# Two weight slots for k and q of four heads, weight loads at the end of a head, and 32-column tiles in the attention burst

## The chip, the core and the metric

The kernel runs on one core of a Trainium2 chip. The time is that of one execution on the device in microseconds (us): the median of 3 runs. TensorE is called PE here, VectorE DVE, ScalarE ACT, GpSimd POOL and SyncE SP. SP computes nothing; it issues nearly all of the DMAs, one after another, and when one of them must wait, everything behind it on SP waits too.

## What is computed

An attention over buckets, followed by two feed-forward layers (`_moe_ref`, `_moe2_ref`), for 2 batches of 768 tokens, 8 heads of 64:

```python
q_bucket = np.sum((q @ proj > 0) * powers, axis=-1)      # 6 bits per query, and per key
scores = np.where(q_bucket[..., :, None] == k_bucket[..., None, :], scale * q @ k.T, -1e9)
attn = exp(scores - max(scores)); attn = attn / (attn.sum(-1) + 1e-09)
x = (attn @ v) as tokens x 512
h = x @ w_in;  x = (h * tanh(softplus(h))) @ w_out       # 512 -> 2048 -> 512
h = x @ w_in2; out = (P(h) / Q(h)) @ w_out2              # the same sizes
```

## The kernel before

All weights come as 64-bit floats and are turned on the chip into two 32-bit parts (hi and lo); x is held in two such parts too.

**Attention** takes 16 heads one after another. The order of all its work is written out by hand: `order` gives each piece of work (by name) a slot, six slots to a head, and within a slot the pieces stand in the table's order. `run` goes through the slots; every engine then executes its own instructions in that order. In slots 0 to 5 of head h, `st(h, c)` makes scores and the exponential E for key tile c (4 matmuls, L405, then ACT L410), and `smax(h+1, c)` the row maxima of the next head (L356, then DVE L360). Slot 5 then holds PE's burst: the bucket products of head h+2 (`code_products`, L307), E times v (`pv`, L295 in `both`, six key tiles) and the sum of E over the keys (`dsum`, L440). These three are plain 32-bit matmuls; each instruction shows as two records. L307 and L295 work in column tiles of 64 (two matmuls side by side), L440 in tiles of 32 (four side by side).

The row maxima of head h+1 reach PE by a detour, called the row write here: DVE turns them (`fin_a`, L367), and `fin_b` writes them with four DMAs of 0.8 KB into one row of `qB` (L373, qB<-stt, two issued by SP, two by ACT). The first `st` matmul of head h+1 reads that row. `fin_b` is issued in slot 5, before the burst.

The other DMAs of a head, all on SP: kk<-qB 384 KB and kk<-qX 192 KB (`move_k`, `move_x`), kq<-kq 384 KB (`load`: k and q of a later head), d<-rc, cs<-dv 3 KB and R<-d 192 KB (`store`, `gather`, `spread`: the reciprocals of the sums, through DRAM), qX<-qB 192 KB (`move_h`), and in every second head vf<-v 384 KB.

**Weights of the first layer.** While attention runs, 7 of the 16 weight tiles (EARLY) are loaded and split, in 14 parts, one to a head: `ring_load` (L121, r<-w, 512 KB), `convert` on DVE (L102, L105, L108), hi and lo on POOL. Part n is converted in slot 5 + 6n (W_AT) and loaded W_LEAD slots earlier. The first SHARED tiles have no slot of their own yet, because their slots `w0` to `w2` hold k and q during attention; their parts are stored to DRAM (`ring_put`, L144, w<-r, 2 x 256 KB in slot 8 + 6n) and loaded back by `first` (L556) near the end of attention, in the slots that FIRST lists. The other parts go straight into their weight slot (`slot_split`).

The feed-forward layers then run in 96 steps; nothing of them is touched.

Of the kernel before, what the change touches and what calls it, by code (L numbers as in the profile page):

```python
# [9 lines left out]
F32 = mybir.dt.float32  # L10
# [8 lines left out]
B, H, S, D = 2, 8, 768, 64  # L19
NT, DM, DFF = B * S, H * D, 2048  # L20
NF = DFF // 128
NK = DM // 128
HALF = S // 2
# [2 lines left out]
NC = S // 128  # L26
BIG = 2.0 ** 40
NBITS = 6
EARLY, SHARED = 7, 3
FIRST = (90, 91, 92, 93), (77, 77, 83, 83), (85, 86, 89, 89)  # L30
W_AT, W_LEAD = 5, 4
POOL_LO = (("lo", 1), ("lo", 2))
ENG = dict(
    lo="dd", hi="aa", xhi="a", xlo="dd", whi="pppp", wlo="pppp",
# [12 lines left out]
def attention_moe_moe(ctx: ExitStack, tc: tile.TileContext, kq, v, proj2, cst, eye, w1, w2, ab, out):  # L47
    nc = tc.nc

    def pool(stack, name, bufs=1, **kw):  # L50
        return stack.enter_context(tc.tile_pool(name=name, bufs=bufs, **kw))
# [3 lines left out]
    wpool = pool(ctx, "w")  # L55
# [119 lines left out]
    def attention(actx, tctx):  # L175
# [22 lines left out]
        p_raw = ac.tile([128, 64], F32, tag="pr", name="pr")  # L198
# [32 lines left out]
            nc.gpsimd.memset(f32(KK[0])[32:33, 0], -1.0)  # L231
            nc.gpsimd.memset(f32(Z), 0.0)

        raws = {}

        def load(h):
            if not 0 <= h < B * H:
                return
            b, hh = divmod(h, H)
            raws[h] = wpool.tile([128, S], F32, tag=f"w{h % 3}", name="kq")  # L240
            nc.sync.dma_start(out=raws[h], in_=kq[b, hh])


# [45 lines left out]
        def qhalf(t, a):  # L289
            return t[:, a * HALF:(a + 1) * HALF]  # L290


        def both(o, w, x, start=False, stop=False):
            for a in range(2):
                nc.tensor.matmul(out=o[64 * a:64 * a + 64, 0:HALF + 2], lhsT=w, rhs=x[:, a], start=start, stop=stop)  # L295

        def halves(p):
            return p[:, :, 0:HALF]
# [4 lines left out]
        ct = {}  # L303

        def code_products(h):
            for a in range(2):
                nc.tensor.matmul(  # L307
                    out=ct[h][a][64 * a:64 * a + 64, 0:HALF], lhsT=p_raw, rhs=qhalf(raws[h], a), start=True, stop=True
                )


        def codes(h):
            if not 0 <= h < B * H:
                return
            p = [two_banks() for _ in range(1 + (h == 0))]
            ct[h] = p[0][:, 0], p[-1][:, 1]
            code_products(h)
# [97 lines left out]
        def pv(h, c):  # L415
            if not 0 <= h < B * H:
                return
            j, e = divmod(h, 2)
            if c == 0:
                pvt[h] = two_banks()[:, 0]  # L420
            both(pvt[h], VF[j % 2][:, e, c], pt[h, c], start=(c == 0), stop=(c == NC - 1))
# [104 lines left out]
        nh = B * H  # L526
        parts = [(f, s) for f in range(EARLY if wide64 else 0) for s in range(PARTS[0])]
        jobs = {}
# [8 lines left out]
        for n, p in enumerate(parts):  # L537
            i = W_AT + 6 * n
            for fn, d in ((ring_load, -W_LEAD), (convert, 0), (ring_out, 1), (ring_put, 3))[:4 if p[0] < SHARED else 3]:
                jobs.setdefault(max(0, i + d), []).append((fn, p))  # L540

        def weights(g):
            for fn in (ring_out, convert, ring_load, ring_put):
# [5 lines left out]
        def first(f, n):  # L549
# [27 lines left out]
            ("code_q", code_q, -7, 1),  # L577
            ("move_x", move_x, -7, 1),
            ("load", load, -25, 1),
            ("first", first, FIRST, -2),  # L580
            ("pv", pv, (5,) * 6, 6),
# [6 lines left out]
            ("xlo", xlo, 29, 0),  # L588
            ("weights", weights, 0, -1),
            ("gather", gather, 6, 1),  # L590
            ("spread", spread, 12, 1),
            ("load_v", load_v, -12, 0),
            ("move_h", move_h, -5, 1),
        )
        last = 6 * nh
        slots = {}
        done = set()
        for name, fn, at, per in order:
            if name == "first":
                todo = [(at[f][n] if f < SHARED else 60, (f, n)) for f in range(EARLY) for n in range(4)]  # L600
            elif name == "pair":
                todo = [(6 * h + c + 1, (h, c)) for h in range(nh) for c in at]
            elif type(at) is tuple:
                todo = [(at[c] + 6 * h, (h, c)) for h in range(nh) for c in range(per)]
            elif per > 0:
                todo = [(at + 6 * h + c, (h, c) if per > 1 else (h,)) for h in range(nh) for c in range(per)]
            elif per == 0:
                todo = [(at + 12 * j, (j,)) for j in range(nh // 2)]
            else:
                todo = [(g, (g,)) for g in range(6 * nh)]  # L610
            for g, k in todo:
                slots.setdefault(max(g, 0), []).append((name, fn, k))
# [269 lines left out]
    with tc.manual_schedule():  # L882
        nc.scalar.preload_act_table_set("natural_log_exp_and_others")
        tctx = ExitStack()
        with ExitStack() as actx:
            run, tail = attention(actx, tctx)
            run()
        with ExitStack() as mctx:
            run = moe(mctx, tctx, tail)
            run()  # L890
# [55 lines left out]
```

## Time and profile before

| | us |
|---|---|
| median of 3 runs | 745.07 (744.18 to 747.27) |
| the profiled execution | 744.9 |
| its span, first to last instruction | 743.1 |
| PE busy | 731.5 (98% of the span) |
| DVE, ACT, POOL busy | 583.5, 426.0, 128.6 |

The granted clock of PE is 1.00 throughout, so nothing here is about the clock. PE is busy almost all the time by its records, but a busy PE is not yet a PE that streams: the end of a matmul is modelled, and records overlap. Where PE stands still shows in the idle time ahead of a row, in square brackets, with what ended it. Line numbers (L295) are those of the kernel before.

### The profile page before, as it was taken

To read this page: it belongs to the slowest core of one execution; us is meant where nothing else is said; L and a number is where in the kernel's file an instruction comes from. 1 tells how busy PE (TensorE), PEld (TensorE's weight loads), DVE (VectorE), ACT (ScalarE), POOL (GpSimd) and SP (SyncE) were. 2 spreads that over 40 slices of the span, in tenths; PEclk is the share of its full clock that TensorE was granted. 3 is DMA by queue.
4 is the path that set the end of the run, shared out by engine and by line. 5 is a ranking of instruction groups with operands and counts; after the bars stand their busy time and mean duration, and the time that the engine had idled before them with its cause. 6 is when DMAs were issued, how large, how long until landed. Compare 5 with 4: busy or idle time off the path is not lost.

```text
span 743.1 us, 10799 instructions
## 1 busy us (share of the span) xinstructions
PE 731.5 (98%) x3764; PEld 579.4 (78%) x3764; DVE 583.5 (79%) x1016; ACT 426.0 (57%) x701; POOL 128.6 (17%) x105
## 2 busy tenths in 40 slices
PE   8999999999999999999999999999999999999997
PEld 5767676767678888888888888878888888888886
DVE  5778989999829995755556777499998888898886
ACT  4766676767564442312123343687877776777674
POOL 6745556565630000000000000000000000000000
PEclk9999999999999999999999999999999999999999
DMA  7766776666554353455555777300000100010001
GB/s 189 194 177 173 214 200 193 158 174 164 140 167 149 120 151 113 120 164 166 147 162 169 243 241 225 107 0 1 1 0 17 41 0 2 0 57 1 0 1 56
DMA packets 45862, 85.49 MB, mean 115 GB/s; under 512 B 7152, under 2 KB 17520, under 8 KB 45808
## 3 DMA queue, kind: packets, MB, share of 16 engines
q1 hardware_dynamic: 45304, 84.75, 38.9%
q8 instruction: 29, 0.48, 0.3%
q14 instruction: 25, 0.20, 0.1%
q10 hardware_dynamic: 504, 0.06, 0.1%
HBM read 57.77 MB, written 14.73 MB: 98 GB/s over the span
## 4 chain that ended last, share of the span: by engine, by line
PE 91%; DVE 4%; DMA 2%; issue 1%; ACT 1%; SPq 0%; POOL 0%; DVEq 0%
PE h L690 34%; PE y L708 17%; PE y L710 17%; PE s L405 9%; PE s L295 6%; PE s L356 5%; PE s L440 2%; DMA qB<-stt 1%; PE s L307 1%; PE s L324 1%; DVE qX L72 1%; DVE smt L360 1%; DMA pr<-proj 0%; DVE xl L718 0%; DVE kk L330 0%
## 5 line engine op out<-in xcount | busy, mean ns | idle before, releaser
L690 PE MATMUL h<-xh,w 128*128 128x512 f32 x768 | 204.9, 389 | 0.0
L690 PEld LDWEIGHTS h<-xh,w 128*128 128x128 f32 x768 | 144.1, 188 | 30.3 <-issue 0.3
L72 DVE TENSOR_TENSOR gl<-ep,gh 128x512 fp32r<-128x512 f32 x96 | 65.9, 686 | 66.2 <-ACT ep L734 65.4
L733 ACT ACTIVATE gh<-h 128x512 fp32r<-128x512 f32 x48 | 28.7, 599 | 150.7 <-PE h L690 137.4
L690 PE MATMUL h<-xl,w 128*128 128x512 f32 x384 | 102.6, 389 | 0.0
L360 DVE TENSOR_REDUCE smt<-s 128x1 fp32r<-128x770 f32 x90 | 86.1, 959 | 19.2 <-PE s L356 14.2
L710 PE MATMUL y<-w,gh 128*128 128x512 f32 x384 | 96.3, 389 | 0.0
L708 PE MATMUL y<-gh,w 128*128 128x512 f32 x384 | 94.8, 389 | 0.0
L430 POOL TENSOR_TENSOR es<-e,e 128x768 f32<-128x768 f32 x48 | 88.8, 1854 | 23.9 <-ACT e L410 23.7
L410 ACT ACTIVATE e<-s 128x768 f32<-128x768 f32 x96 | 77.5, 814 | 22.1 <-PE s L405 21.6
L708 PEld LDWEIGHTS y<-gh,w 128*128 128x128 f32 x384 | 72.1, 188 | 15.0
L690 PEld LDWEIGHTS h<-xl,w 128*128 128x128 f32 x384 | 72.1, 188 | 15.0
L710 PEld LDWEIGHTS y<-w,gh 128*128 128x128 f32 x384 | 72.1, 188 | 15.0
L295 PE MATMUL s<-e,vf 128*64 128x386 f32 x384 | 65.1, 488 | 0.0
L740 ACT ACTIVATE ep<-h 128x512 f32<-128x512 f32 x48 | 28.6, 595 | 52.4 <-PE h L690 52.4
L108 DVE SCALAR_TENSOR_TENSOR r<-r,t 128x256 int32<-128x256 int32 (+1 forms) x114 | 52.1, 457 | 4.8
L405 PE MATMUL s<-qB,kk 128*128 128x384 f32 x192 | 50.4, 343 | 5.4 <-DMA qB<-stt 3.5
L105 DVE SCALAR_TENSOR_TENSOR t<-r,t 128x256 int32<-128x256 int32 (+1 forms) x114 | 52.2, 458 | 3.9
L742 DVE TENSOR_TENSOR n<-n,ep 128x512 f32<-128x512 f32 x48 | 33.1, 690 | 26.9 <-ACT n L741 26.9
L295 PEld LDWEIGHTS s<-e,vf 128*64 128x64 f32 x384 | 27.4, 137 | 34.4 <-issue 34.0
L710 PE MATMUL y<-w,gl 128*128 128x512 f32 x192 | 53.3, 392 | 0.5 <-DVE gl L72 0.4
L708 PE MATMUL y<-gl,w 128*128 128x512 f32 x192 | 51.3, 389 | 0.0
(82 smaller groups left out, 1013.9 us busy)
## 6 DMA issues: line engine op xcount, KB each, us to landing
r<-w SPq DMA_DIRECT2D x100, 256.0 KB
w<-r SPq DMA_DIRECT2D x64, 128.0 KB
w<-w SPq DMA_DIRECT2D x16, 512.0 KB
r<-w SPq DMA_DIRECT2D x14, 512.0 KB
kq<-kq SPq DMA_DIRECT2D x16, 384.0 KB
kk<-qB SPq DMA_DIRECT2D x15, 384.0 KB
kk<-qX SPq DMA_DIRECT2D x16, 192.0 KB
qX<-qB SPq DMA_DIRECT2D x16, 192.0 KB
```

The lines of the kernel that those rows point to most:

```text
L72: nc.vector.tensor_tensor(out=o, in0=i, in1=f32(h), op=ALU.subtract)
L105: lambda: nc.vector.scalar_tensor_tensor(out=t, in0=r[:, :, 1], scalar=-0x40000000, in1=t, op0=ALU.bitwise_and, op1=ALU.bitwise_or),
L108: lambda: nc.vector.scalar_tensor_tensor(out=o, in0=r[:, :, 0], scalar=29, in1=t, op0=ALU.logical_shift_right, op1=ALU.bitwise_or),
L295: nc.tensor.matmul(out=o[64 * a:64 * a + 64, 0:HALF + 2], lhsT=w, rhs=x[:, a], start=start, stop=stop)
L356: nc.tensor.matmul(out=p[:, a, 0:HALF], lhsT=qB[h % NB][:, c * 128:(c + 1) * 128], rhs=qhalf(KK[h % NB][:, 0], a), start=True, stop=True,)
L360: nc.vector.tensor_reduce(out=m, in_=p[:, :, 0:HALF + 1], op=ALU.max, axis=AX.XY)
L405: nc.tensor.matmul(out=p[:, a, 0:HALF], lhsT=kk[:, c * 128:(c + 1) * 128], rhs=qq[:, a * HALF:(a + 1) * HALF], start=(i == 0), stop=(i == 1),)
L410: nc.scalar.activation(out=E[c][:, :, 0:HALF], in_=halves(p), func=ACT.Exp, scale=1.0 / D ** 0.5)
L430: nc.gpsimd.tensor_tensor(out=sums[h, c], in0=halves(pt[h, c]), in1=halves(pt[h, c + 1]), op=ALU.add)
L690: nc.tensor.matmul(out=p, lhsT=w[:, c * 128:(c + 1) * 128], rhs=x[:, c, :], start=(n == 0), stop=(n == 11))
L708: nc.tensor.matmul(out=y[m], lhsT=w[:, DM + m * 128:DM + (m + 1) * 128], rhs=g, **s)
L710: nc.tensor.matmul(out=y[m], lhsT=g[:, m * 128:(m + 1) * 128], rhs=w[:, DM:2 * DM], **s)
```

## The change

- `load` puts head h into half of one of two slots: heads 0 and 1 (mod 4) share `w0`, heads 2 and 3 share `w1`. `w2` is free from the start, so SHARED goes from 3 to 2, and tile 2 (parts 4 and 5) goes straight into its slot. FIRST loses its first entry: tile 0 takes the slots in which tile 1 was loaded, tile 1 those of tile 2.
- W_LEAD goes from 4 to 6: a part is loaded in slot 5 of the head before, behind `fin_b`, `move_k`, `move_x`, `load` and `store`, instead of slot 1. The stores (slot 8 + 6n) stay.
- `spread` (R<-d) goes from slot 0 to slot 2 of a head, behind the stores.
- `both` and `code_products` make four matmuls of 32 columns where there were two of 64.

```diff
-EARLY, SHARED = 7, 3
-FIRST = (90, 91, 92, 93), (77, 77, 83, 83), (85, 86, 89, 89)
-W_AT, W_LEAD = 5, 4
+EARLY, SHARED = 7, 2
+FIRST = (77, 77, 83, 83), (85, 86, 89, 89)
+W_AT, W_LEAD = 5, 6
...
-            raws[h] = wpool.tile([128, S], F32, tag=f"w{h % 3}", name="kq")
+            i, j = divmod(h % 4, 2)
+            if h < 4 and j == 0:
+                home[i] = wpool.tile([128, 2, 2 * DM], F32, tag=f"w{i}", name="kq")
+            raws[h] = home[i][:, j, 0:S]
...
-            for a in range(2):
-                nc.tensor.matmul(out=o[64 * a:64 * a + 64, 0:HALF + 2], lhsT=w, rhs=x[:, a], start=start, stop=stop)
+            for a in range(4):
+                nc.tensor.matmul(
+                    out=o[32 * a:32 * a + 32, 0:HALF + 2], lhsT=w[:, a % 2 * 32:a % 2 * 32 + 32], rhs=x[:, a // 2],
+                    start=start, stop=stop,
+                )
...
-                jobs.setdefault(max(0, i + d), []).append((fn, p))
+                jobs.setdefault(max(1, i + d), []).append((fn, p))
...
-            ("spread", spread, 12, 1),
+            ("spread", spread, 14, 1),
...
+            elif name == "spread":
+                todo = [(min(at + 6 * h, last + 6), (h,)) for h in range(nh)]
```

`code_products` is changed as `both` is. On SP, this is what stands between the store of the reciprocals (d<-rc) and the row write (qB<-stt) in a head that also stores a weight part, before:

```order
L491 DMA d<-rc 24x32
L475 DMA cs<-dv 24x1x32
L501 DMA R<-d 64x768
L121 DMA r<-w 128x1024
L287 DMA qX_133<-qB_130 64x768
L144 DMA w_1_619<-r 128x512 x2
L373 DMA qB_130<-stt_124 1x6x32 x2
```

and the same head now (the lines of the file have moved by 3 to 7: L373 is L380 there):

```order
L498 DMA d<-rc 24x32
L121 DMA r<-w 128x1024
L482 DMA cs<-dv 24x1x32
L290 DMA qX_133<-qB_130 64x768
L144 DMA w_1_661<-r 128x512 x2
L508 DMA R<-d 64x768
L380 DMA qB_130<-stt_124 1x6x32 x2
```

The load r<-w has moved ahead, R<-d from ahead of the stores to behind them. Heads that store a part are now four (parts 0 to 3), and were six.

On PE, the burst at the end of a head, before (e is E, es the pairwise sums of E):

```order
L356 MATMUL s_118<-kk_136,qB_130 128x384 x2
L307 MATMUL s_119<-kq,pr 64x384 x2
L295 MATMUL s_116<-e_98,vf_139 64x386 x2
...
L295 MATMUL s_116<-e_103,vf_139 64x386 x2
L440 MATMUL s_117<-es,ones 32x192 x12
L405 MATMUL s_118<-qB_130,kk_136 128x384 x2
```

and now:

```order
L363 MATMUL s_118<-kk_136,qB_130 128x384 x2
L313 MATMUL s_119<-kq,pr 32x384 x4
L298 MATMUL s_116<-e_98,vf_139 32x386 x4
...
L298 MATMUL s_116<-e_103,vf_139 32x386 x4
L447 MATMUL s_117<-es,ones 32x192 x12
L412 MATMUL s_118<-qB_130,kk_136 128x384 x2
```

The whole burst now stands in one tile size; it has 40 instructions where it had 26, and the order is the same.

## Rows read from the trace of the kernel before

**Rows 1.** Busy time by stretch: us; PE, PEld, DVE, ACT, POOL busy (instructions); clock; DMA share; GB/s.
```profile
23.80:215.10 191.30, 185.88 (x1351) 131.68 (x1347) 159.10 (x217) 130.15 (x206) 112.52 (x75) 1.00 0.63 175
215.10:743.20 528.10, 523.68 (x2304) 431.97 (x2304) 409.55 (x776) 282.43 (x478) 0.00 (x0) 1.00 0.29 89
```

**Rows 2.** Timeline of PE, burst of head 11: start, us, line, operation, records.
```profile
163.57 0.87 PE L307 MATMUL s<-kq,pr 128*64 128x384 f32 x4
164.27 4.06 PE L295 MATMUL s<-e,vf 128*64 128x386 f32 x24
168.26 1.18 PE L440 MATMUL s<-es,ones 128*32 128x192 f32 x24
...
169.37 0.62 PE L405 MATMUL s<-qB,kk 128*128 128x384 f32 x2
```

**Rows 3.** Timeline of PE, starts of heads 3 to 8: [idle before <- what ended it].
```profile
52.31 1.18 PE L440 MATMUL s<-es,ones 128*32 128x192 f32 x24
55.06 0.59 PE L405 MATMUL s<-qB,kk 128*128 128x384 f32 x2 [1.56 <-DMA qB<-stt]
...
69.11 0.59 PE L405 MATMUL s<-qB,kk 128*128 128x384 f32 x2 [1.77 <-DMA qB<-stt]
...
81.61 0.59 PE L405 MATMUL s<-qB,kk 128*128 128x384 f32 x2 [0.21 <-DMA qB<-stt]
...
95.12 0.59 PE L405 MATMUL s<-qB,kk 128*128 128x384 f32 x2 [1.23 <-DVE r L108]
...
107.78 0.59 PE L405 MATMUL s<-qB,kk 128*128 128x384 f32 x2 [0.38 <-DVE t L105]
...
120.33 0.59 PE L405 MATMUL s<-qB,kk 128*128 128x384 f32 x2 [0.27 <-DVE t L105]
```

**Rows 4.** Chain that ended last, 62 to 70 us: start, us, what.
```profile
63.83 5.15 DMA qB<-stt
```

**Rows 5.** Timeline of SP's queue in head 3: start, us of issue, DMA, count.
```profile
55.56 0.88 SPq L491 DMA_DIRECT2D d<-rc  x1
...
60.10 0.50 SPq L501 DMA_DIRECT2D R<-d  x1
60.66 0.57 SPq L121 DMA_DIRECT2D r<-w  x1
61.34 0.48 SPq L287 DMA_DIRECT2D qX<-qB  x1
61.91 1.01 SPq L144 DMA_DIRECT2D w<-r  x2
63.02 1.53 SPq L373 DMA_DIRECT2D qB<-stt  x2
```

**Rows 6.** Who waited for whom on SP's queue: total us, times, longest.
```profile
SPq L501 <- DMA d<-rc: 24.0, 15, 2.9
```

**Rows 7.** Busy time by stretch, head 3 (columns as in rows 1).
```profile
58.40:61.00 2.60, 2.60 (x17) 2.60 (x16) 2.43 (x4) 2.15 (x3) 2.38 (x2) 1.00 0.03 8
61.00:66.00 5.00, 5.00 (x32) 2.14 (x30) 4.85 (x8) 2.07 (x4) 2.71 (x2) 1.00 0.86 255
```

**Rows 8.** Timeline of SP's queue in head 11.
```profile
161.14 0.55 SPq L121 DMA_DIRECT2D r<-w  x1
...
164.95 1.57 SPq L373 DMA_DIRECT2D qB<-stt  x2
```

**Rows 9.** DMA issues: DMA, queue, count, KB each.
```profile
r<-w SPq DMA_DIRECT2D x14, 512.0 KB
...
w<-r SPq DMA_DIRECT2D x12, 256.0 KB
```

**Rows 10.** Timeline of PE's weight loads, same burst: second and last pair of L295.
```profile
164.27 0.14 PEld L295 LDWEIGHTS s<-e,vf 128*64 128x64 f32 x2 [0.18 <-issue]
...
167.51 0.14 PEld L295 LDWEIGHTS s<-e,vf 128*64 128x64 f32 x2 [0.18 <-issue]
```

**Rows 11.** Timeline of DVE, first row maxima of head 12.
```profile
170.79 6.10 DVE L360 TENSOR_REDUCE smt<-s 128x1 fp32r<-128x770 f32 x6 [0.29 <-PE s L356]
```

More of the change, by code (lines that the diff above doesn't have):

```diff
@@ L232, in memsets @@
             nc.gpsimd.memset(f32(Z), 0.0)
-        raws = {}
+        raws, home = {}, {}
         def load(h):
@@ L305, in code_products @@
         def code_products(h):
-            for a in range(2):
+            for a in range(4):
                 nc.tensor.matmul(
-                    out=ct[h][a][64 * a:64 * a + 64, 0:HALF], lhsT=p_raw, rhs=qhalf(raws[h], a), start=True, stop=True
+                    out=ct[h][a // 2][32 * a:32 * a + 32, 0:HALF], lhsT=p_raw[:, a % 2 * 32:a % 2 * 32 + 32],
+                    rhs=qhalf(raws[h], a // 2), start=True, stop=True,
                 )
```

## The prediction

> **What bounds the kernel now.** I read the stretches first. The feed-forward part, 528.1 us, has PE busy for 523.7 and no DMA to speak of; nothing of it is changed, and I leave it at its time [rows 1]. The heads take 191.3 us with PE busy 185.9: 5.4 us of PE's records are missing there, while DVE is busy for 159.1 and the DMA engines for 63% [rows 1]. So the question is where in a head PE stands, and how tight its burst is.
>
> Then the timeline of PE around the bursts. An undisturbed one (head 11) goes from L307 at 163.57 to L295 at 164.27, L440 at 168.26 and the next head's first matmul at 169.37: 0.70, 3.99 and 1.11 us [rows 2]. In heads 3 to 8 the last step is longer, with PE idle for 1.56, 1.77, 0.21, 1.23, 0.38 and 0.27 us [rows 3], together 5.42. For the first of them the starts say 55.06 - 52.31 = 2.75 against 1.11, an excess of 1.64, 0.08 more than the idle time; with 0.07 more on each of the six the stalls cost 5.84 us. No other head shows such a row.
>
> What they wait for is the row write. Three rows name it [rows 3], and the chain has it at 5.15 us from issue to landing [rows 4]. The other three name DVE's weight conversion (L108, L105), which is no input of that matmul; I take them for the row write too, since all six heads in a row follow on each other and the heads after them show neither.
>
> Why is a DMA of 0.8 KB so late? In head 3, SP issues d<-rc at 55.56, then cs<-dv, and cannot issue R<-d before 60.10 [rows 5]: R reads d back from DRAM and waits for it to land; all heads together SP lost 24.0 us in 15 such waits [rows 6]. Meanwhile the DMA engines are idle (share 0.03 from 58.4 to 61.0 [rows 7]). Behind the wait everything goes out at once: R 192, r 512, qX 192 and the two stores 2 x 256 KB, 1408 KB from 60.10 on, with the row write right behind them at 63.02 [rows 5]. At 255 GB/s [rows 7] these 1.44 MB need 5.65 us, to 66.7, and the row write, behind them in the queues, lands at 63.83 + 5.15 = 68.98. Without its stall of 1.77 + 0.07 PE would have started at 69.11 - 1.84 = 67.27 [rows 3]. In head 11, without stores, the load goes out at 161.14, the row write's issues end at 164.95 + 1.57 = 166.52 [rows 8], and PE starts at 169.37 without waiting [rows 2]: with a short queue it lands in 2.9 us or less behind its last issue.
>
> **The change part by part.** The sum is made against the profiled execution, 744.9 us; the median of the runs is 745.07, so I add 0.2 at the end.
>
> *Loads at the end of a head, R behind the stores, fewer stores.* Nothing now waits on SP between cs and the stores except for landings of DMAs long issued: d has two further DMAs and two stores ahead of R in which to land. So in a head like head 3 the 512 KB load goes out at about 56.4, right behind d, and qX, stores and R by about 59.5, as SP needs some 0.5 us for each [rows 5]. The engines, free from 58.4 on [rows 7], then have the same 1408 KB done some 2.6 us earlier, near 64.1, about when the row write is issued; it lands 2.9 us or less after that, inside the time that PE has. In a head that also loads v, 384 KB (1.5 us at the same rate) are added, and two of the four heads that still store do so; I leave 0.3 us of stall to each of these. The two heads whose stores vanish (six stores were 12 rows of 256 KB [rows 9], four of these go, and as many loads near the end) are as heads 9 and later. So 5.84 - 0.6 = 5.2 us come back. Bounds: 5.84 at most; at least what followed on the two vanished stores (idle 1.23 and 0.38, and the one after them, 0.27 [rows 3]), 1.88 + 3 x 0.07 = 2.1. I take the value near the upper end, because both causes, the blocked SP and the burst that follows, are moved in all heads.
>
> The load moved behind the row write delays cs<-dv, which stands behind it now: 512 KB at 255 GB/s is 2.1 us. Its reader, the reciprocal on DVE, is at the end of the next head, one head (12.25 us) later; that cover is the whole of a head, and if it were gone DVE would stand for those 2.1 us with a row maximum behind it. R two slots later is read by DVE near the end of that same head; in head 3 it went out at 60.10 because of the wait, and now at about 59.5, so nothing is later. The conversion gets its data two slots earlier; POOL splits as many parts as before. The shared slots ask nothing of PE: k and q of a head are loaded when the slot half was read a whole head earlier instead of in the same slot. Tiles 0 and 1 are loaded in slots in which tiles 1 and 2 were, which were in time.
>
> *The burst in tiles of 32.* The 24 records of L295 are 12 pairs; from the second to the last pair's load there are 10 steps in 167.51 - 164.27 = 3.24 us, 0.324 a pair [rows 10]. Twelve pairs need 3.89, and L295 takes 3.99 until L440 starts [rows 2]: 0.10 us is lost where tiles of 64 give way to tiles of 32. With one size in the whole burst this goes. L307 takes 0.70 for two pairs, 0.05 over 2 x 0.324; half of it, I estimate, is the wider first load. So 0.10 to 0.15, I take 0.13 a head, 16 heads: 2.1 us. The streams themselves stay as long: four matmuls side by side instead of two, each as many columns. That four keep step is what L440 shows: 24 records of 192 columns, six groups of four, in 1.11 us including its own exit [rows 2], 0.185 a group or 0.96 ns a column, against 0.324 / 386 = 0.84 ns for a pair. As 1.11 contains the change to full-width tiles (some 0.1, as above), a group of four is as fast as a pair. Bounds from these rows: -2.4 us (0.15 gained), or, if all 1.11 were stream, (0.96 - 0.84) x 386 x 12 = 0.56 us lost a head, less the 0.13: 0.43 x 16 = +6.9. I take -2.1.
>
> The Trainium skill speaks against this edit: TensorEngine Tiling (Array Packing), Performance Considerations, Instruction Overhead, gives each matmul some 60 cycles of its own. The burst has 14 more instructions, 28 more records a head, 448 in all; at 2.4 GHz that would be an estimated 11.2 us, and the whole change 744.9 - 5.2 - 2.1 + 11.2 = 748.8, on the side of rival (3); I give it 1 in 100. The trace does not bear it out for tiles side by side: 24 such overheads (0.6 us) and 6 x 192 columns at 0.84 ns (0.97) would be 1.57, and L440 takes 1.11 [rows 2].
>
> *Sum.* 744.9 - 5.2 - 2.1 = 737.6, and 737.8 as a median.
>
> **Rivals.** (1) *Only the vanished stores help.* The stores of four heads still stand just ahead of the row write, and the bytes are the same; if the queue is as full as before in these heads, 3.75 us of stalls stay. For it: the stores' place. Against: the idle DMA engines at 58.4 to 61.0. Time: 744.9 - 2.1 - 2.1 = 740.7, median 740.9. (2) *DVE becomes the bound.* In head 12 its first row maximum waits 0.29 us for PE [rows 11]; a burst 0.13 shorter leaves 0.16, and less in heads with a larger part of x to split. If it has no slack elsewhere, the 2.1 us stay in: 739.7, median 739.9. Against: four PSUM buffers let it lag by a matmul or two. (3) *Slower: four streams do not keep step at 386 columns.* There are 14 groups a head now (12 and 2), 224 in all; each nanosecond over 0.324 us costs 0.22 us, so the change is slower than before from 33 ns a group on (0.357). By the bound above it would be 744.9 - 5.2 + 6.9 = 746.6, and, were the four done as two pairs, 224 x 0.324 = 73 us more; L440's rows speak against both. Time: 746.6 and more, median 746.8 at the nearest bound. (4) *The stalls only move:* loads of k and q now queue with the weight load, and another wait comes up at the head's start as long as the old ones; only the burst gains: 742.8, median 743.0.
>
> **How the numbers follow.** Forecast 0.62, (1) 0.17, (2) 0.10, (3) 0.07, (4) 0.04. A measurement of this kernel tells about 0.5%, 3.7 us, from no change: faster is below 741.3. The forecast (0.61 of its 0.62) and (2) (0.09) lie below it, (1) by a little, some 0.10 of its 0.17; (4) does not. Faster 0.61 + 0.10 + 0.09 = 0.80. Of (3), which begins at 746.8 and has no near end, 0.06 lies over 748.8: slower 0.06. The rest, 0.14, is the same. The range: below, all stalls and 0.15 a head give 744.9 - 5.84 - 2.4 + 0.2 = 736.9, and runs spread by a microsecond or so around a median, hence 735.5; above, it takes in (1) and (2), to 742.0. (3) and (4) stay out.
>
> **What would show it.** L298's 48 records a head in about 3.9 us, and L447 starting on the step of a group, no 0.1 later; the first L412 of heads 3 to 8 without idle time, or 0.3 us in heads 3 and 5; PE idle in the heads below 1 us in all; no wait of SP for d<-rc before the stores; DMA engines busy between cs<-dv and the stores and emptier before the row write. It is wrong if L298's steps are longer than 0.33 us a group, if the stalls stand at other heads or other lines, or if DVE's row maxima stop waiting for PE.

## The result and the profile after

The changed kernel takes 737.52 us (737.04 to 737.98, 6 runs) against 745.22 (744.18 to 747.27, 6 runs) for the kernel before: a ratio of 0.9894, with a 95% interval of 0.988 to 0.9908. The prediction was 737.8. The total came out 0.3 us from it, but its terms did not: the order of the DMAs gave all that was expected and a little more, the smaller tiles gave less than half, and the rest of the agreement lies in the start of the kernel, which was not forecast. That part of it is luck.

The profiled execution took 737.73 us, its span 735.9. The stretches of the kernel after, in the columns of [rows 1], are first the heads, from the first L298 to the feed-forward part, and that part; then three pieces of head 3:

```profile
23.07:207.84 184.77, 184.77 (x1789) 129.04 (x1781) 159.82 (x217) 128.34 (x206) 112.12 (x75) 1.00 0.63 172
207.84:736.00 528.16, 523.74 (x2308) 431.97 (x2304) 409.82 (x776) 282.90 (x478) 0.00 (x0) 1.00 0.28 89
...
53.50:57.50 4.00, 4.00 (x25) 3.86 (x24) 3.43 (x4) 3.37 (x5) 3.15 (x3) 1.00 0.97 307
57.50:60.30 2.80, 2.80 (x29) 1.77 (x31) 2.60 (x5) 2.36 (x3) 2.56 (x2) 1.00 0.79 254
60.30:63.20 2.90, 2.90 (x44) 1.15 (x40) 2.87 (x5) 0.19 (x1) 1.11 (x1) 1.00 0.04 12
```

The heads took 191.23 us up to the first feed-forward matmul, L690 at 215.03 ([rows 1] cuts 0.07 later), and take 184.77, 6.46 less; 0.73 went ahead of the first L298 (23.80 to 23.07); the feed-forward part is unchanged (528.1 us in both). In the heads PE is now busy for the whole stretch. The DMA engines, idle before the burst of transfers and full during the row write [rows 7], are full from 53.5 on (share 0.97) and empty (0.04) when the row write goes out at 60.31. SP's queue in the same head shows why (start, us of issue, DMA, count):

```profile
52.55 0.89 SPq L498 DMA_DIRECT2D d<-rc  x1
53.50 0.35 SPq L121 DMA_DIRECT2D r<-w  x1
53.97 0.61 SPq L482 DMA_DIRECT2D cs<-dv  x1
54.70 0.51 SPq L290 DMA_DIRECT2D qX<-qB  x1
55.71 0.85 SPq L144 DMA_DIRECT2D w<-r  x2
56.66 0.66 SPq L508 DMA_DIRECT2D R<-d  x1
60.31 1.56 SPq L380 DMA_DIRECT2D qB<-stt  x2
```

The load r<-w follows d<-rc at once instead of 5.1 us later [rows 5], the stores go out before R<-d, and SP has issued everything 3 us before the row write. In the table of waits (total us, times, longest) PE has no wait for qB<-stt left, and SP's wait for d<-rc has fallen from 24.0 us [rows 6] to 9.5, which delays no row write that PE waits for:

```profile
PE s L331 <- DVE s L220: 1.2, 1, 1.2
PE s L313 <- DMA pr<-proj: 0.8, 1, 0.8
PE y L719 <- DVE gl L72: 0.4, 1, 0.4
...
SPq L508 <- DMA d<-rc: 9.5, 11, 1.7
```

PE's timeline (start, us, line, operation, records) at the starts of heads 3 and 4, and then one whole burst with what follows it:

```profile
51.27 1.16 PE L447 MATMUL s<-es,ones 128*32 128x192 f32 x24
52.36 0.62 PE L412 MATMUL s<-qB,kk 128*128 128x384 f32 x2
...
63.49 1.16 PE L447 MATMUL s<-es,ones 128*32 128x192 f32 x24
64.58 0.62 PE L412 MATMUL s<-qB,kk 128*128 128x384 f32 x2
...
156.67 0.85 PE L313 MATMUL s<-kq,pr 128*32 128x384 f32 x8
157.34 4.07 PE L298 MATMUL s<-e,vf 128*32 128x386 f32 x48
161.23 1.16 PE L447 MATMUL s<-es,ones 128*32 128x192 f32 x24
162.32 0.62 PE L412 MATMUL s<-qB,kk 128*128 128x384 f32 x2
```

Heads 3 and 4 start 1.09 us after their L447, where head 3 took 2.75 [rows 3]; so do all others from head 1 on. The burst's three steps are 0.67, 3.89 and 1.09 us against 0.70, 3.99 and 1.11 [rows 2]: to three places 0.669, 3.890, 1.088 against 0.696, 3.990, 1.113, so it is 0.152 us shorter. But from head to head an undisturbed head went from 12.25 us only to 12.21 to 12.23; only the first two keep the whole gain (12.09 us each). Where the other 0.11 went stands in the scores that follow, in PE's weight loads of this head:

```profile
163.37 0.30 PEld L412 LDWEIGHTS s<-qB,kk 128*128 128x128 f32 x2
...
164.53 0.30 PEld L412 LDWEIGHTS s<-qB,kk 128*128 128x128 f32 x2 [0.15 <-ACT e L417]
```

The first matmul of the third score tile waits for ACT's exponential (L417) to free a buffer. Its step, the thirteenth of the head, lasts 0.25 to 0.28 us in heads 2 to 14 instead of 0.175; in heads 0 and 1 it is 0.174. In ACT's own timeline the exponential stands at the end of a row of five jobs that begins with a wait for DVE:

```profile
160.76 1.16 ACT L346 ACTIVATE qB<-s,cst 32x384 fp32r<-32x384 f32 x2 [2.80 <-DVE kk L337]
161.95 0.17 ACT L463 ACTIVATE vb<-s 128x1 f32<-128x1 f32 x1
162.15 1.17 ACT L465 ACTIVATE ev<-s,vb 64x384 f32<-64x384 f32 x2
163.35 0.42 ACT L474 ACTIVATE dv<-s,bias 128x192 f32<-128x192 f32 x1
163.67 1.53 ACT L417 ACTIVATE e<-s 128x768 f32<-128x768 f32 x2
```

The same row was there in the kernel before, in head 11:

```profile
167.64 1.17 ACT L339 ACTIVATE qB<-s,cst 32x384 fp32r<-32x384 f32 x2 [2.77 <-DVE kk L330]
...
170.54 1.69 ACT L410 ACTIVATE e<-s 128x768 f32<-128x768 f32 x2
```

Counted from the burst's first matmul, the first exponential starts at 170.54 - 163.57 = 6.97 us before [rows 2] and at 163.67 - 156.67 = 7.00 after. By these two heads it does not depend on how long the burst is. PE came to the scores 0.15 us sooner and waited for it.

One group of the page (busy, mean ns, idle time and what ended it):

```profile
L367 DVE TENSOR_REDUCE smt<-s 128x1 fp32r<-128x770 f32 x90 | 86.4, 960 | 12.2 <-PE s L363 4.6
```

### The profile page after: what moved, and what is told of

Read it like the earlier page. It is cut to its first block, busy times and chain, and to the rows that moved or that the text cites. A ratio compares the mean times of both kernels' runs of the same rounds, so it can differ in the third digit from the quotient of the medians.

```text
span 735.9 us, 11670 instructions
## 1 busy us (share of the span) xinstructions
PE 729.6 (99%) x4212; PEld 576.7 (78%) x4212; DVE 584.4 (79%) x1016; ACT 424.5 (58%) x701; POOL 128.2 (17%) x105
## 4 chain that ended last, share of the span: by engine, by line
PE 95%; DVE 3%; issue 1%; ACT 1%; DMA 0%
PE h L699 33%; PE y L717 17%; PE y L719 16%; PE s L412 10%; PE s L298 8%; PE s L363 5%; PE s L447 2%; PE s L313 2%; PE s L331 1%; DMA pr<-proj 0%; DVE w L72 0%; DVE ep L769 0%; DVE ep L767 0%; DVE xl L727 0%; DVE n L768 0%
## 5 line engine op out<-in xcount | busy, mean ns | idle before, releaser
L72 DVE TENSOR_TENSOR gl<-ep,gh 128x512 fp32r<-128x512 f32 x96 | 66.0, 687 | 67.1 <-ACT ep L743 66.4
L437 POOL TENSOR_TENSOR es<-e,e 128x768 f32<-128x768 f32 x48 | 88.8, 1861 | 16.7 <-ACT e L417 16.3
L417 ACT ACTIVATE e<-s 128x768 f32<-128x768 f32 x96 | 76.4, 813 | 17.2 <-PE s L412 16.6
L298 PE MATMUL s<-e,vf 128*32 128x386 f32 x768 | 65.2, 487 | 0.0
L298 PEld LDWEIGHTS s<-e,vf 128*32 128x32 f32 x768 | 24.8, 110 | 37.0 <-issue 36.2
```

The lines of the kernel that those rows point to most:

```text
L72: nc.vector.tensor_tensor(out=o, in0=i, in1=f32(h), op=ALU.subtract)
L298: nc.tensor.matmul(out=o[32 * a:32 * a + 32, 0:HALF + 2], lhsT=w[:, a % 2 * 32:a % 2 * 32 + 32], rhs=x[:, a // 2], start=start, stop=stop,)
L417: nc.scalar.activation(out=E[c][:, :, 0:HALF], in_=halves(p), func=ACT.Exp, scale=1.0 / D ** 0.5)
L437: nc.gpsimd.tensor_tensor(out=sums[h, c], in0=halves(pt[h, c]), in1=halves(pt[h, c + 1]), op=ALU.add)
```

## The experiments

The heads' stretch, from the first L298 to the feed-forward part, leaves out the start, which differs between kernels; so it stands beside each time. For the kernel before it is 191.23 us by the same bounds. It is one profile of each kernel; the three of the changed kernel agree within 0.01 us. Ratios are against the kernel before on the same chip, with 95% intervals.

| kernel | us | ratio | heads, us |
|---|---|---|---|
| changed kernel again, twice | 737.05, 737.6 | 0.9892 [0.9868, 0.9915], 0.99 [0.9882, 0.9917] | 184.76, 184.76 |
| tiles of 32 alone | 744.93 | 0.9999 [0.9976, 1.0021] | 191.51 |
| all but the tiles | 738.69 | 0.9916 [0.9891, 0.9941] | 185.70 |
| shared slots alone | 742.95 | 0.9969 [0.9949, 0.9989] | 190.21 |
| order alone (load early, R late) | 738.39 | 0.9914 [0.9888, 0.9939] | 185.77 |
| load early alone | 739.32 | 0.9917 [0.989, 0.9943] | 185.73 |
| R late alone | 738.99 | 0.9915 [0.9888, 0.9941] | 186.01 |
| changed, qX a head part earlier | 737.57 | 0.9894 [0.987, 0.9918] | 184.70 |
| changed, key codes first, qX earlier | 735.81 | 0.9876 [0.9857, 0.9895] | 183.23 |
| changed, key codes first | 735.74 | 0.9875 [0.9856, 0.9894] | 183.51 |
| all but the tiles, key codes first | 739.1 | 0.9921 [0.9904, 0.9938] | 185.43 |

**The tiles alone.** The kernel before with `both` and `code_products` in four matmuls of 32 columns.

> The kernel before with the 32-column tiles alone (loads, stores, slots and R as they were). Theory A (the burst gains 0.15 us a head, but from the second head on PE then waits for ACT at the third score tile and gives about 0.12 back; in heads 3 to 8 the row write sets the start anyway; the start of the kernel gains 0.7): span 743.1 - 0.7 - 0.3 to 0.5 = 741.9 to 742.1, with the idle time before L405 at heads 3 to 8 about 0.15 us longer each. Theory B (the burst's 2.4 us all arrive, as the prediction had it): 740.0 to 741.0.

PE's waits for the row write stay at three stalls of together 5.3 us:

```profile
PE s L409 <- DMA qB<-stt: 5.3, 3, 2.7
```

The time shows no gain, with an interval of 1.8 us less to 1.6 more; the span of 742.7 us is above what either theory gave. The stalls did not each grow by 0.15 us: they stand at other heads (1.61 us at head 3, 0.11 at 4, 2.66 at 5, 1.02 at 7). And there is a loss that neither theory has. Behind the longest one the granted clock of PE falls (columns as in [rows 1]):

```profile
81.20:84.60 3.40, 3.40 (x11) 3.40 (x12) 1.93 (x3) 0.81 (x1) 1.90 (x2) 0.50 0.94 202
```

PE had stood still for 2.66 us until 81.18. Then it ran at 0.50, the lower of its two levels (1.2 GHz), and at 1.00 again from 84.7 on. This head took 13.67 us from start to start (81.18 to 94.85), and undisturbed ones here take 12.22. So 1.4 us of the 191.51 are the clock's. What the tiles alone are worth without it stays open; a shorter burst that lets PE arrive earlier at a wait for the row write is part of the account, not all of it.

**All but the tiles.** The changed kernel with `both` and `code_products` as before.

> The changed kernel with the 64-column tiles of before in both places; slots, loads, stores and R as changed. Theory A: all stalls of heads 3 to 8 gone (5.9 us), the start as before: span 743.1 - 5.9 = 737.2, 1.3 above the changed kernel. Theory B (the burst is worth 2.1 to 2.4): 738.0 to 738.4 and some stalls left.

No stall, heads of 12.25 to 12.28 us, 185.70 us in all, as theory A had it. Against the changed kernel's 184.77 the tiles give 0.93 us on top of the order. In time the intervals of their ratios overlap, so the 0.93 rests on the profiles.

**Shared slots alone.** The two slots for k and q, with the loads and R<-d at their old places.

```diff
-W_AT, W_LEAD = 5, 6
+W_AT, W_LEAD = 5, 4
...
-            ("spread", spread, 14, 1),
+            ("spread", spread, 12, 1),
```

> The kernel before with the two shared slots alone: SHARED 2, four heads' k and q in two slots, FIRST without its first entry; load in slot 1, R in slot 0, 64-column tiles as before. Theory A (the row write is late because SP stands still for d and then sends load and stores at once just ahead of it): stalls at heads 3, 4, 5 stay (3.7 us), those at heads 6 and 7 shrink to what heads with a load and v have (0 to 0.3): span 743.1 - 2 = 741 to 741.5. Rival (only the vanished bytes matter, as in rival 1 of the prediction): the same here, 741.0, but then the kernel with the order alone must not gain. Rival C (the number of stores matters through the whole queue, each store less shortens all later stalls): 738 to 740.

Its PE timeline has two of the old stalls left, and head 4, which follows the second, takes 13.78 us:

```profile
52.75 0.59 PE L408 MATMUL s<-qB,kk 128*128 128x384 f32 x2 [0.38 <-DMA qB<-stt]
...
67.44 0.59 PE L408 MATMUL s<-qB,kk 128*128 128x384 f32 x2 [2.40 <-DMA qB<-stt]
...
81.22 0.62 PE L408 MATMUL s<-qB,kk 128*128 128x384 f32 x2
```

No wait stands in that head. The clock does (columns as in [rows 1]):

```profile
66.00:68.90 2.90, 1.46 (x8) 1.49 (x9) 0.77 (x2) 0.67 (x2) 1.91 (x2) 1.00 0.91 198
68.90:72.30 3.40, 3.40 (x12) 3.40 (x12) 1.84 (x2) 1.77 (x3) 1.67 (x1) 0.51 0.38 127
```

After PE had stood still for 2.40 us it fell to the lower level, as with the tiles alone, and the head lost 13.78 - 12.25 = 1.53 us. In the profile of the kernel before, whose longest stall is 1.77 us, it stays at 1.00. But over the executions of the kernels with stalls the mean granted clock goes down to 0.995 (before and tiles alone) and 0.997 (shared slots alone), and with the order alone or one of its halves it is never under 0.999. So a stall can cost more than the time that PE stands.

In time the shared slots gave 0.0031 x 744.36 = 2.3 us (0.8 to 3.8 by the interval), near the 2.1 that the prediction took for the two vanished stores. In the heads they gave 1.02 us: the idle time at the starts fell from 5.42 to 2.78 us, and the clock took 1.53 back. The stalls at heads 3 and 4, behind stores that remain, stay; the one at head 5, which theory A kept, is gone.

**The order alone, and its halves.** The kernel before with only the loads two slots earlier and R<-d two slots later; then each by itself.

```diff
-W_AT, W_LEAD = 5, 4
+W_AT, W_LEAD = 5, 6
...
-            ("spread", spread, 12, 1),
+            ("spread", spread, 14, 1),
```

> The kernel before with the order on SP alone: W_LEAD 6 and R in slot 14, three shared tiles and six stored parts, 64-column tiles. Theory A: stalls of heads 3 to 8 nearly all gone, also where stores stay (heads 6 and 7 too): span 737.2 to 738.0. Rival (1) of the prediction (only the vanished stores help): 743.1, no change.

> The kernel before with W_LEAD 6 alone (load at the end of a head); R stays in slot 0, ahead of the stores, so SP still stands for d. Theory A: 192 + 192 + 512 KB instead of 1408 KB go out in the burst ahead of the row write, 2 us less of queue, so most of the stalls go and some stay in heads with stores and v: span 737.2 to 738.5. Rival (SP's standing for d is the cause by itself): stalls stay, 741 to 743.

> The kernel before with R behind the stores alone (slot 14); load stays in slot 1. Theory A: SP does not stand, the same 1408 KB go out about 2.5 us earlier, all stalls go: span 736.6 to 737.5. Rival (the load next to the stores is the cause): stalls stay, 740 to 743.

All six stores are still there, and no stall is left but one of 0.3 us in the last of the three. The order alone takes the heads to 185.77; each half does nearly the same. The rivals by which the stalls stay are out. With the load early alone, SP still waits for d before R<-d in head 3, from 55.82 to 58.70:

```profile
55.20 0.62 SPq L475 DMA_DIRECT2D cs<-dv  x1
58.70 0.50 SPq L501 DMA_DIRECT2D R<-d  x1
59.29 0.54 SPq L287 DMA_DIRECT2D qX<-qB  x1
```

With R late alone, the load follows at once and everything but R has been issued by 57.6:

```profile
55.31 0.43 SPq L121 DMA_DIRECT2D r<-w  x1
55.85 0.58 SPq L287 DMA_DIRECT2D qX<-qB  x1
56.52 1.05 SPq L144 DMA_DIRECT2D w<-r  x2
58.25 0.48 SPq L501 DMA_DIRECT2D R<-d  x1
60.64 1.57 SPq L373 DMA_DIRECT2D qB<-stt  x2
```

So it takes the blocked SP and the 512 KB load behind it together to make the row write late. Either move is enough.

**The changed kernel again.** The mark for the next kernel, on its chip.

> The changed kernel once more, beside the next ones on one chip: 0.989 of before, span 735.5 to 736.2.

**qX earlier.** An attempt to let ACT's row begin sooner, by moving DVE's product qX (L72) out of the way.

```diff
-            ("lo", lo, -7, 1),
+            ("lo", lo, -13, 1),
```

> The changed kernel with one piece of work moved: the split of k and q into their low part (lo on DVE) is made six slots earlier, in the same place of DVE's sequence but for the head after. Theory A (since the shorter burst, PE waits at the third score tile of each head for ACT, which is late because the query codes on ACT, L346, must wait for lo and the key codes on DVE, and the copies out of PSUM and the first exponentials stand behind them): ACT makes the codes about 2 us earlier, the third tile's wait goes, a head takes 12.10 instead of 12.22 us, span 735.9 - 13 x 0.115 = 734.4. Rival (PE waits there for DVE's row maxima, or for the change of tile size): nothing changes, 735.9; if lo early delays the row write, slower.

```profile
160.99 1.17 ACT L346 ACTIVATE qB<-s,cst 32x384 fp32r<-32x384 f32 x2 [2.78 <-DVE kk L337]
```

The idle time ahead of L346 is unchanged: what it waits for, the second L337, still stood behind a qX in DVE's row, that of the head after. The time is unchanged too (737.57 us). The kernel says nothing on the theory.

**Key codes first.** The same with the second half of the key codes ahead of qX; then that exchange alone; then that exchange with tiles of 64.

```diff
-            ("lo", lo, -7, 1),
             ("code_kb", lambda h: code_k(h, (1,)), -7, 1),
+            ("lo", lo, -7, 1),
```

> The changed kernel once more, as the mark for the three beside it on the same chip: 737.1 to 737.5, heads of 12.21 to 12.23 us, the 13th step of a head's scores at 0.25 to 0.28 us instead of 0.175.

> The changed kernel with DVE's second copy of the key codes (L337) put ahead of the product qX (L72), which itself keeps a slot six groups earlier. ScalarE's query codes (L346) wait for that copy (idle 2.80 us <-DVE kk L337), and the codes, the evictions and the first exponential (L417) stand in one row on ScalarE behind it. Theory A (what the tiles gave is handed back because the third score tile waits for that row): L346 starts 1.4 us earlier, the first exponential some 0.2 to 0.3 us earlier, the 13th step falls to 0.175 us, a head to 12.10 to 12.13 us, and sixteen heads come to 1.4 to 1.9 us less: 735.2 to 736.0. Theory B (the long 13th step is for the score buffers or the tiles themselves, not for ScalarE's row): L346 starts earlier but the step stays at 0.25 us or more and the time stays at 737.1 to 737.5.

> As the one before it, but qX keeps its slot and only the two DVE instructions change places. Theory A: L346 starts 1.4 us earlier here too, so the same gain, 735.2 to 736.0, unless qX, now up to 0.6 us later, is waited for. Theory B: 737.1 to 737.5.

> The same exchange of the two DVE instructions with the burst in tiles of 64 columns, the order of the changed kernel kept. There the 13th step waits for nothing (0.177 us), so theory A: no gain against the same kernel without the exchange, 738.4 to 738.7, heads of 12.25 to 12.28. If it is faster too, by a microsecond or more, the exchange helps by another way than the one theory A says. Theory B has no gain either.

ACT, PE's weight loads and the heads' stretch in the kernel with the exchange alone. In this head the burst starts at 155.29 and the scores at 160.94:

```profile
158.80 1.16 ACT L346 ACTIVATE qB<-s,cst 32x384 fp32r<-32x384 f32 x2 [2.21 <-DVE qX L72]
...
162.00 0.81 ACT L417 ACTIVATE e<-s 128x768 f32<-128x768 f32 x1
```

```profile
162.96 0.36 PEld L412 LDWEIGHTS s<-qB,kk 128*128 128x128 f32 x2
```

```profile
22.67:206.18 183.51, 183.29 (x1789) 129.91 (x1781) 152.39 (x217) 130.45 (x206) 113.09 (x75) 1.00 0.64 174
```

The first exponential now starts 162.00 - 155.29 = 6.71 us after the burst's start instead of 7.00, the weight load of the third tile comes without idle time, the thirteenth step is 0.174 us, and 10 of the first 13 head-to-head times are 12.09 us (the others are 12.12, 12.38, where PE waited 0.2 us for the row write, and 12.06 behind it). On the same chip 735.74 us (735.38 to 736.02) stand against 737.6 (736.76 to 738.2) for the changed kernel. With tiles of 64 the same exchange makes no such gain: 739.1, heads of 12.25, 185.43 us in all against 185.70 without the exchange. So the gain is what the tiles had handed back, as the first theory said: with the exchange, tiles of 32 are worth 185.43 - 183.51 = 1.92 us in the heads, and without it 0.93. The rest of the difference in time (739.1 against 735.74) lies outside the heads. These two versions with tiles of 32 beat both kernels.

The way is not the one that the theory had. With the exchange alone L346 still waits for qX, by its row above (qX reads qB, which L346 writes). It starts 158.80 - 155.29 = 3.51 us after the burst's start instead of 160.76 - 156.67 = 4.09, so 0.58 sooner and not 1.4. That is the 0.57 us by which qX itself is shorter in this kernel; why it is, the last section shows. Only where qX is made a head earlier as well does L346 wait for the second L337 alone, and there it starts 1.2 us sooner (157.65, burst at 154.76). Both give the same time: ACT's next job, L463, reads what L298 wrote and starts 4.81 us after the burst's start in both (160.10 and 159.57).

## Why the prediction was right, and where not

**The cause of the stalls** held. With the order alone the heads go from 191.23 to 185.77, 5.46 us. The 5.84 of stalls are gone and heads are 0.02 to 0.03 longer here and there. That the three stalls under DVE's name were the row write's too holds: in heads 6, 7 and 8 its last DMA landed at 94.92, 107.55 and 120.19, 0.14 to 0.23 us ahead of PE's start. The forecast was 5.2; the 0.3 us left to heads 3 and 5, where stores and a v load meet, did not appear. The landing behind the last issue, "2.9 us or less", was 1.3 to 1.7 from the issue's end. The lower bound of 2.1 for the vanished stores measured 2.3 by itself in time; in the profile 2.6 us of idle time went, and the clock took 1.5 of them back. The prediction prices a stall at the time that PE stands and has no term for the clock behind it. What I did not see is that the two moves are not two contributions: each alone gives 5.2 to 5.5 us.

**The burst's own size** held: 0.13 us a head was forecast with 0.15 as its bound, and 0.152 was measured. The group step stayed at 0.324 us, 3.89 / 12, with four matmuls side by side, so rival (3) did not occur. The 448 more records cost nothing in that step. By that row the overhead of each matmul that the Trainium skill states (TensorEngine Tiling (Array Packing), Instruction Overhead) does not show. L447 follows 3.89 us after L298's start instead of 3.99, 0.10 sooner, now that no tiles of 64 stand ahead of it. The Trainium skill (TensorEngine Tiling (Array Packing), Tiling Modes, Key Properties) says that a change of mode drains TensorE. The trace agrees with that.

**The term that was mis-sized** is the one that multiplied this by 16: "2.1 us". On top of the order the tiles gave 0.93 us in the profiles (185.70 to 184.77), and without the order no gain that shows. From head 2 on about 0.11 us of each head's 0.15 went into the wait for ACT. Where that wait is gone, with the key codes first, the tiles give 1.92 us: the size of a burst was right, and the step that failed is that each burst's gain reaches the next head. Rival (2) had the right idea, that another engine takes the gain, but the wrong engine. I looked at DVE's 0.29 us of slack at the first row maximum [rows 11] and did not ask what sets ACT's first exponential, though its row, with no idle time from L339 to L410, was in the trace. DVE did come close to its bound: its row maxima waited 4.6 us for PE instead of 14.2. But it was not late, since its first maximum of this head starts 0.62 us after PE's L363 both in the changed kernel (163.12, 163.74) and in the one with the key codes first (161.74, 162.36), where the wait for PE on the page is back at 14.0 us.

**The sum** came out at 737.52 against 737.8 because an error made up for another. The heads gave 6.46 us, not 7.3. The start gave 0.73 in the one profile of before beside the one of after, and the prediction had it at nothing. The first L298 starts at 22.9 to 23.1 in three profiles of the changed kernel, at 23.80 before, at 23.11 with the tiles alone, at 23.84 with the load early alone, at 22.75 with the order alone, and at 22.41 to 23.21 in the others; no edit orders these numbers, so I ascribe the 0.73 to none. What sets the start stays open.

**Rivals** (1) and (4) are out: the stalls went in all six heads, with all stores in place, and no new wait at the row write came up in the changed kernel.

## What to carry to other kernels

Before a shorter stretch of the busiest engine is multiplied by the number of rounds, look for what the next stretch waits for at its second or third step, and whether that hangs on the stretch or on a row of another engine that starts independently of it. If that row has no idle time in it, the gain ends there, and an exchange of two instructions on a third engine can release it, here because it moved one of them clear of a fourth engine's work. Before a wait is priced, look at the granted clock behind it as well. On a queue that issues in order, move the transfer that waits for another's landing behind everything that does not; one such move can be worth as much as moving all the bytes.

## What the runs showed that I had not expected

DVE's product qX takes 1.50 us a head in the changed kernel and 0.94 in the two with the key codes first, with the same shape and count (line, operation, count, busy, mean ns). First the changed kernel:

```profile
L72 DVE TENSOR_TENSOR qX<-kq,qB 128x768 fp32r<-128x768 f32 x13 | 19.6, 1505 | 0.0
```

and then the one with the exchange alone:

```profile
L72 DVE TENSOR_TENSOR qX<-kq,qB 128x768 fp32r<-128x768 f32 x13 | 12.2, 936 | 0.0
```

The timelines show what lies beside it. In the changed kernel POOL's product of two tiles (L437) runs until 159.15 while qX starts at 158.46:

```profile
155.30 3.85 POOL L437 TENSOR_TENSOR es<-e,e 128x768 f32<-128x768 f32 x2
...
158.46 1.50 DVE L72 TENSOR_TENSOR qX<-kq,qB 128x768 fp32r<-128x768 f32 x1
```

With the key codes first, qX starts at 157.77, when POOL has just ended:

```profile
155.94 1.83 POOL L437 TENSOR_TENSOR es<-e,e 128x768 f32<-128x768 f32 x1 [0.23 <-ACT e L417]
...
157.77 0.94 DVE L72 TENSOR_TENSOR qX<-kq,qB 128x768 fp32r<-128x768 f32 x1
```

Standing still until POOL's end and running 0.94 us from there would end qX at 160.09; it ended at 159.96. The Trainium skill says so (SBUF — State Buffer, SBUF: two separate sides): a DVE operation with two inputs in SBUF and a GpSimd one that reads SBUF share a pair of ports, and whichever comes second stands until the first has ended. The trace agrees within 0.13 us. Thirteen heads of 0.57 us are 7.4 us of DVE's time, 159.82 to 152.39 in the heads. With tiles of 64 qX is shorter by as much (1490 to 935 ns), but the heads are only 0.27 us shorter (185.70 to 185.43): no score tile waits for ACT's row there. With tiles of 32 and the exchange alone it is what brings that row forward.

The row write's own time depends on what stands ahead of it, even for the half that ACT issues on its own queue. Behind the 1.4 MB of head 3 that SP had issued, SP's last DMA of 0.8 KB took 5.15 us from issue to landing [rows 4] and ACT's last one 5.20; in the changed kernel, behind idle DMA engines, the same two took 2.05 and 1.74 us.
